# The second token half of a second DFT, done as four extra chunk pairs of a fast block product, with token forms summed in DRAM

## The chip, the core and the metric

The kernel runs on one core of one Trainium2 chip. The metric is the device time of one execution in microseconds, as the median of three runs: 2019.68 us for the kernel before (2019.68 to 2019.91). The engines are named as in the profile: PE multiplies matrices, DVE and ACT do elementwise work, POOL (GpSimd) does elementwise work and issues accumulating transfers, SP issues plain transfers.

## The reference

`x` is 2048 tokens by 512, in fp32. Two branches are mixed per token by a gate:

```
g = sigmoid((x * gate_w).sum(-1))
a = x @ Wd_re.T ; b = x @ Wd_im.T            # DFT along the hidden axis
A = Ws_re @ a - Ws_im @ b                    # DFT along the tokens, real part
logits = x @ w_gate ; gates = softmax(all 8 logits)
B = sum over e of gates[e] * (silu(x @ w1[e]) @ w2[e])     # 8 experts, 512 -> 1376 -> 512
out = g * A + (1 - g) * B
```

All eight experts take every token (top 8 of 8), so the expert branch is two dense products with 8 x 1376 = 11008 inner rows, that is 86 chunks of 128.

## The kernel before

**Precision.** Every fp32 operand is split into a high part (ACT copies it to the reduced type `F32R`) and a low part (DVE or POOL subtracts the high part from the source). `mm` then issues three matmuls for each product, high by high, low by high and high by low, one matmul in each of L349, L352 and L353. A tile of [128 x 512] or [128 x 1024] therefore costs one ACT and one DVE instruction before PE may read it.

**Stages on PE.** One, the token DFT, in eight phases (`phases`, `plan_left_x`, `plan_right`, `dft`); it comes first here, its results `u` (real and imaginary part, four token blocks of 512) go to DRAM as `ud`, and 10 small matmuls (`warm`, `WARM`) run on constant data before the first operands have landed. Two, the hidden DFT (`plan_y`): for each of the four token blocks `gi`, 8 row blocks of `u` (4 real, 4 imaginary) by 4 output blocks by 3 matmuls, 96 matmuls a token block; DVE multiplies the results by `g` and stores them in `yd`. Three, the expert's first product in 29 rounds (`plan_round`) of three chunks each (two in the last): a fast 20-product scheme on blocks; it reads 20 forms of `x` (`XFORM`, blocks of `x` or sums and differences of two blocks), which are made once, during the hidden DFT and the first round, and stay in SBUF. ACT applies silu, DVE multiplies by the gate rows, and four kinds of hidden activations go to DRAM as `hd`. Four, the expert's second product: pairs of chunks (43 of them) in a seven-product scheme (`FORMS`, numbers 1 to 7 in four groups `GROUPS`), each product with two token halves `hf` and two output row blocks `n`, 3 matmuls each. `add_to` adds the seven products into eight accumulators, which start from `yd`; `store` writes them out.

**What sets the order.** The token DFT's events have times written by hand (`ev`). From the hidden DFT on, `Plan` puts every instruction into an order by a list schedule: each has a due time, a duration constant, a release time and buffers from rings (`XF`, `WF`, `RA`, `RW`, `T`, `PS`); tables (`XDUE`, `RAWRING`, `SUMRING`, `NRAW`, `NX`) set due times and rings of the x forms. PE, ACT, DVE and POOL each then run their own instructions strictly in that order; SP issues loads and stores in its order too, and each waits for its buffer.

**Names that the change and the prediction touch.** `xq` is the sum of two x blocks for the token DFT's fifth product, made by DVE in `s1`; `plan_right` sets when the low parts of the DFT matrix are made (`lo`); `raw_block` loads the x blocks for the forms; `add_to` starts an accumulator; `plan_pair_w` and `plan_pair_h` load and split weights and activations for a pair of chunks; `plan_unit` issues a product's matmuls. T1 is the planned start of the rounds, T2 that of the second product.

## Time and profile before

| what | value |
|---|---|
| median of three runs | 2019.68 us |
| the profiled execution, its own time | 2020.08 us |
| its span, first to last instruction | 2018.3 us |
| matmul records on PE | 8836 |
| PE busy | 2006.9 us, 99% |
| DVE / ACT / POOL busy | 1659.0 / 1030.1 / 861.9 us |
| token DFT on PE | to 322.2 us |
| hidden DFT on PE | 322.2 to 409.2 us |
| 29 rounds | 409.2 to 1194.6 us |
| second product | 1194.6 to 2013.5 us |

PE matmuls are pipelined; what counts for the time is the distance of their starts, not the length of a record. The waits are idle time on an engine, put down to the instruction that released it. PEclk in a table of stretches is the share of TensorE's full clock that was granted.

### The profile page before, as it was taken

The numbers are of one execution on the slowest core, as the hardware profiler recorded it, in microseconds if no ns is written. First come the engines' busy times: TensorE is split into PE (matmuls) and PEld (weight loads), VectorE is DVE, ScalarE is ACT, GpSimd is POOL, SyncE is SP. The second block draws the span as 40 slices with busy tenths as digits, with TensorE's granted clock in tenths as the row PEclk, the third lists the DMA queues.
The fourth block names the chain that finished last, engine by engine and source line by source line (L and its number), as shares of the span: only waits on it lengthen the run. The fifth ranks groups of instructions, "written<-read, shape, count | busy, mean of one in ns | idle before, by whom it ended". The sixth has DMA issues, their size and how long they took to land. (4 is left out here: it accounts for less than half of the span.)

```text
span 2018.3 us, 26838 instructions
## 1 busy us (share of the span) xinstructions
PE 2006.9 (99%) x8836; PEld 1655.3 (82%) x8836; DVE 1659.0 (82%) x1929; ACT 1030.1 (51%) x1440; POOL 861.9 (43%) x829
## 2 busy tenths in 40 slices
PE   9999999999999999999999999999999999999999
PEld 7887888888888888888878888888888888888887
DVE  8998996887878887887778786687778888899875
ACT  6544453455555555555555565544445444445442
POOL 0000000188889888889798830000002221235330
PEclk9999999999999999999999999999999999999999
DMA  8676696545565546454645599899889988999991
GB/s 317 214 254 237 221 311 214 190 148 183 175 201 172 185 157 213 166 190 166 221 152 178 178 317 368 298 333 287 268 265 286 293 269 262 279 279 331 303 291 45
DMA packets 205236, 475.20 MB, mean 235 GB/s; under 512 B 22788, under 2 KB 37508, under 8 KB 205096
## 3 DMA queue, kind: packets, MB, share of 16 engines
q1 hardware_dynamic: 192280, 450.15, 64.9%
q0 software_dynamic: 12672, 23.07, 6.9%
q8 instruction: 69, 1.13, 0.2%
q14 instruction: 71, 0.58, 0.1%
q10 hardware_dynamic: 144, 0.26, 0.1%
HBM read 366.36 MB, written 107.03 MB: 235 GB/s over the span
## 5 line engine op out<-in xcount | busy, mean ns | idle before, releaser
L1198 ACT ACTIVATE psp<-psp 128x512 f32<-128x512 f32 x280 | 160.3, 582 | 208.5 <-DVE psp L1182 141.8
L1182 DVE TENSOR_TENSOR psp<-psp,tc 128x512 f32<-128x512 f32 x79 | 55.3, 699 | 33.9 <-PE psp L353 27.9
L1260 ACT ACTIVATE tc<-psp 128x512 f32<-128x512 f32 x88 | 52.4, 597 | 42.7 <-PE psp L353 32.9
L1097 POOL TENSOR_TENSOR tc<-ras 128x256 f32<-128x256 f32 x27 | 20.0, 739 | 121.9 <-DMA ras<-w_dram 120.4
L1427 POOL DMA_DIRECT2D xfx1n<-w_dram x11 | 9.9, 963 | 132.3 <-DVE xf211n L1484 94.8
L1260 ACT ACTIVATE tg<-psp 128x512 f32<-128x512 f32 x67 | 40.0, 598 | 35.4 <-PE psp L353 27.3
L1182 DVE TENSOR_TENSOR psp<-psp,tg 128x512 f32<-128x512 f32 x52 | 36.3, 699 | 21.8 <-PE psp L353 17.8
L340 POOL TENSOR_TENSOR c73011l<-cb,c73011h 128x1024 fp32r<-128x1024 f32 x1 | 2.4, 2412 | 116.8 <-ACT c73011h L346 116.8
L1112 POOL TENSOR_TENSOR wfs1nn<-tc,wfs1nn 128x512 fp32r<-128x512 f32 x32 | 42.0, 1313 | 15.4 <-ACT wfs1nn L1110 8.9
L1208 DVE TENSOR_TENSOR tc<-psp,tc 128x512 f32<-128x512 f32 x62 | 42.5, 685 | 5.2 <-ACT psp L1198 4.2
L1097 POOL TENSOR_TENSOR tc<-tc,ras 128x256 f32<-128x256 f32 x54 | 43.1, 797 | 4.2 <-DVE xfx13n L997 1.8
L1112 POOL TENSOR_TENSOR wfs3n<-tc,wfs3n 128x512 fp32r<-128x512 f32 x29 | 38.4, 1326 | 10.9 <-ACT wfs3n L1110 10.9
L1112 POOL TENSOR_TENSOR wfs2n<-tc,wfs2n 128x512 fp32r<-128x512 f32 x29 | 39.0, 1344 | 8.2 <-ACT wfs2n L1110 8.1
L346 ACT ACTIVATE c<-cd 128x512 fp32r<-128x512 f32 x32 | 20.2, 633 | 38.7 <-DVE cd L343 38.7
L1260 ACT ACTIVATE tw<-psp 128x512 f32<-128x512 f32 x41 | 24.5, 597 | 30.3 <-PE psp L353 23.3
L1182 DVE TENSOR_TENSOR psp<-psp,tw 128x512 f32<-128x512 f32 x37 | 25.9, 699 | 16.4 <-PE psp L353 14.4
L1112 POOL TENSOR_TENSOR wfs0n<-tc,wfs0n 128x512 fp32r<-128x512 f32 x26 | 35.3, 1356 | 7.8 <-ACT wfs0n L1110 7.4
L349 PE MATMUL psp<-xfx,wfs0n 128*128 128x512 f32 x94 | 36.6, 389 | 0.0
L353 PE MATMUL psp<-xfx,wfs0n 128*128 128x512 f32 x94 | 36.6, 389 | 0.0
L340 POOL TENSOR_TENSOR c12111l<-ca,c12111h 128x1024 fp32r<-128x1024 f32 x1 | 2.6, 2602 | 78.4 <-PE u L353 78.4
L1112 POOL TENSOR_TENSOR wfs0n<-tg,wfs0n 128x512 fp32r<-128x512 f32 x24 | 32.1, 1339 | 7.4 <-ACT wfs0n L1110 7.4
L1112 POOL TENSOR_TENSOR wfs3n<-tg,wfs3n 128x512 fp32r<-128x512 f32 x24 | 33.0, 1373 | 3.4 <-ACT wfs3n L1110 3.3
(3474 smaller groups left out, 7980.9 us busy)
## 6 DMA issues: line engine op xcount, KB each, us to landing
hd<-tc SPq DMA_DIRECT2D x161, 256.0 KB, 2.3
ca<-cT_dram SPq DMA_DIRECT2D x63, 512.0 KB, 5.4
hd<-tg SPq DMA_DIRECT2D x108, 256.0 KB, 2.5
hd<-tw SPq DMA_DIRECT2D x75, 256.0 KB, 2.3
...
```

Source lines behind the costliest of these rows:

```text
L340: pin(nc.gpsimd.tensor_tensor(*a))
L346: pin(nc.scalar.activation(dst, src, f, **kw))
L349: ins = nc.tensor.matmul(ps, lh, rh, start=start, stop=False, skip_group_check=True)
L353: nc.tensor.matmul(ps, ll, rh, start=False, stop=stop, skip_group_check=True)
L1097: pin(ins.tensor_tensor(low(b, j), src(x), src(y), o))
L1112: lambda: pin(nc.gpsimd.tensor_tensor(r(w)[:, 1, :], f(b), f(w)[:, 0, :], sub)), [oh] + deps, [b, w],
L1182: q = op("DVE", V, due, lambda: pin(nc.vector.tensor_tensor(f(dst), f(a[0]), f(b_[0]), o)), [a[1], b_[1]] + list(deps), [dst, a[0], b_[0]] ...
L1198: os = op("ACT", A, due, lambda: pin(nc.scalar.activation(f(dst), f(src_), AF.Silu, scale=sign)), [o0], [dst, src_])
L1208: oh = op("DVE", V, due + 1.2, lambda: pin(nc.vector.tensor_tensor(f(hb), f(dst), f(gb), OP.mult)), [os, og], [hb, dst, gb], lock=dst.ring ...
L1260: o = op("ACT", AP_, after(x), lambda: pin(nc.scalar.activation(f(b), f(bank[x[0]]), AF.Copy)), [prod[x]], [b, bank[x[0]]])
L1427: return op("POOL", 0.9, due, lambda: pin(nc.gpsimd.dma_start(f(src_)[:, j, :], block(key), accum_op=add, max_dma_last_dim=4096)), deps, [ ...
```

## The change

The four parts, in the order of the program:

- **Start.** 17 warm-up matmuls instead of 10. In the first phase of the token DFT, the sum `xq` of chunks 4 to 7 is made by a plain load from SP and an accumulating transfer from POOL, instead of a DVE instruction. The low parts of the DFT matrix are given an earlier time in all chunks of this phase, not in one alone.
- **x forms.** Twelve of the twenty forms are sums of two blocks. Each is now written to DRAM once (`xs`): a DRAM-to-DRAM copy from SP, then an accumulating transfer from POOL, spread over the phases from the fourth on. The form is then one load. To have only sums there, signs of forms are moved: into ACT's scale and a DVE scalar_tensor_tensor for the low part, into the weight forms (add becomes sub and the other way round) and into silu's scale.
- **Hidden DFT.** It runs for the first two token blocks only, and ACT copies its results to `yd` without a gate; a DVE multiplication by `g` follows when an accumulator is started. The second token half (blocks 2 and 3) is done in the second expert product: the four row-block pairs of `u`, multiplied by `g`, and the DFT weights are appended as pairs 43 to 46, with `hf` = 1 alone, so 2 units in place of 4 a product (`u_row`, `plan_ht`, `half`). Accumulators of that half start from the first product, by an ACT copy. `TILES` says where the added weight tiles (22, 23, and half of 21) stand in each group.
- **Rounds.** A round of three leftover chunks now holds one mixed chunk and the last chunks of two neighbouring experts.

```diff
-WARM = 10
+WARM = 17
...
-        out += pure[e]
-        if e % 2:
-            out.append(mixed[e // 2])
-    return out + [tuple(rest[-2:])]
+        out += [tuple(e * FULL + 3 * i + j for j in range(3)) for i in range(FULL // 3)]
+        if e % 2 == 0:
+            out.append((E * FULL + e // 2, e * FULL + FULL - 1, (e + 1) * FULL + FULL - 1))
+    return out + [(NCHUNK - 2, NCHUNK - 1)]
...
+
+NPAIR2 = NPAIR + ND
+NB2 = (NPAIR2 + 1) // 2
...
-XFORM = {16: "+21", 6: "+11-21", 7: "+13", 13: "+14", 9: "+22-13", 3: "+22", 0: "-14-21", 10: "+23-22",
-         14: "+21+24", 4: "+13-23", 11: "+14-24", 17: "+13-12", 18: "+13+21", 12: "-11-14",
-         15: "+21+23", 1: "+12-22", 19: "+24-22", 5: "+12-14", 2: "-11-13", 8: "+22-14"}
...
+XFORM = {16: "-21", 6: "+xa", 7: "+13", 13: "+14", 9: "+22-13", 3: "+22", 0: "+21-14", 10: "+xb",
+         14: "+xc", 4: "-xd", 11: "-xe", 17: "+xf", 18: "+13-21", 12: "-xg",
+         15: "+xh", 1: "-xi", 19: "+xj", 5: "-xk", 2: "-xl", 8: "+22-14"}
+
+XSUM = {"xa": ("11", "21"), "xb": ("23", "22"), "xc": ("21", "24"), "xd": ("13", "23"), "xe": ("14", "24"), "xf": ("13", "12"),
...
+NRAW, NX, NRW = 4, 20, 9
...
+TILES = ((*range(9), 22, *range(9, 13), 23, *range(13, 17), 21, *range(17, 21)),
+         (*range(14), 22, *range(14, 17), 23, 17, 18, 21, 19, 20),
+         (*range(9), 22, *range(9, 13), 23, *range(13, 17), 21, *range(17, 21)),
+         (*range(9), 22, *range(9, 13), 23, *range(13, 17), 21, *range(17, 21)))
...
+            if j == 2:
+                v["q"] = xp.tile([P, 256], F32, tag="x", name=f"xq{k}_0")
+                nc.sync.dma_start(v["q"], x[k][:, j, :])
+            else:
+                pin(nc.gpsimd.dma_start(v["q"], x[k][:, j, :], accum_op=add, max_dma_last_dim=4096))
...
+        if k < 4:
+            ev(s5 - 3.3, s1)
+        else:
+            ev(s - 12.5, plus, 2)
+            ev(s - 8.5, plus, 3)
...
+    def x_sum(n, k, blk):
+        d, t = int(blk[0]) - 1, int(blk[1]) - 1
+        src_ = xT[2 * d:2 * d + 2, :, t * GT:(t + 1) * GT]
+        if k == 0:
+            nc.sync.dma_start(xs[n], src_)
+        else:
+            pin(nc.gpsimd.dma_start(xs[n], src_, accum_op=add, max_dma_last_dim=4096))
...
-                plan_right(pr, c, ph, k, s - 14, s - 2.9, r, lo=s - 3.4 if k == 2 else None)
+                plan_right(pr, c, ph, k, s - 14, s - 2.9, r, lo=s - 3.4)
...
+        if (pr, c, ph) == (0, 1, "Y"):
+            for n, blocks in enumerate(XSUM.values()):
+                for k, blk in enumerate(blocks):
+                    ev(T + XSUM_AT[0] * n + XSUM_AT[1] * k, x_sum, n, k, blk)
...
-    T1 = T + NG * TG
+    T1 = T + 2 * TG
...
-            oy = op("DVE", V, end + 1 + 0.8 * q,
-                    lambda q=q, t=t: pin(nc.vector.tensor_tensor(f(t), f(banks[q]), f(gy), OP.mult)),
-                    [o, og], [t, gy, banks[q]])
...
+            oy = op("ACT", AP_, end + 1 + 0.8 * q,
+                    lambda q=q, t=t: pin(nc.scalar.activation(f(t), f(banks[q]), AF.Copy)), [o], [t, banks[q]])
...
-    for gi in range(NG):
+    for gi in range(2):
...
+    def x_block(blk):
+        if blk in XSUM:
+            return xs[list(XSUM).index(blk)]
...
+    def second(dst, src, hi, neg):
+
+        if neg:
+            return nc.vector.scalar_tensor_tensor(dst, src, -1.0, hi, OP.mult, sub)
+        return nc.vector.tensor_tensor(dst, src, hi, sub)
...
-            oh = op("ACT", A2 if k is None else A, xdue[m] - 1.4, lambda h=h, s_=s_, k=k: pin(
-                nc.scalar.activation(r(h) if k is None else r(h)[:, k, :], part(s_, k), AF.Copy)),
+            oh = op("ACT", A2 if k is None else A, xdue[m] - 1.4, lambda h=h, s_=s_, k=k, neg=neg: pin(
+                nc.scalar.activation(r(h) if k is None else r(h)[:, k, :], part(s_, k), AF.Copy, scale=-1.0 if neg else 1.0)),
...
+            sign = -sign if j == 1 else sign
...
+    for gi in (2, 3, 0, 1):
+        g = Buf("T")
+        gates2[gi] = (g, load(T2 + 6, lambda g=g, gi=gi: gate_row(f(g), slice(0, P), E, gi), MB, bufs=[g], rel=T2))
...
+            if hf == 0:
+                oy = load(due - 16, lambda: nc.sync.dma_start(f(b), yd[i, a]), 2 * MB,
+                          deps=[ydone[i, a, n] for n in range(2)], bufs=[b], rel=due - 30)
+                g, og = gates2[a]
+                oy = op("DVE", V2, due - 10, lambda: pin(nc.vector.tensor_tensor(
+                    f(b), f(b), f(g)[:, None, :].to_broadcast([P, 2, GT]), OP.mult)), [oy, og], [b, g], lock=True)
+                acco[hf, i, a] = [[oy], [oy]]
+        if not acco[hf, i, a][n]:
+            q = op("ACT", AP_, due, lambda: pin(nc.scalar.activation(acc(hf, i, a, n), f(src), AF.Copy,
+                                                                     scale=1.0 if o == add else -1.0)),
...
+    order2 = [[p for q in tiles for p in (2 * q, 2 * q + 1) if p < NPAIR2] for tiles in TILES]
...
+    def u_row(n, k, dst, due, rel):
+
+        c, d, (k, a) = n // 2, 2 * (n % 2), k
+        g, og = gates2[2 + a]
+        b, view = dst
+        o = load(due - 6, lambda: nc.sync.dma_start(view(), ud[c, 2 + a, d + k]), MB, bufs=[b], rel=rel)
+
+        def go():
+            if c:
+                pin(nc.vector.scalar_tensor_tensor(view(), view(), -1.0, f(g), OP.mult, OP.mult))
+            else:
+                pin(nc.vector.tensor_tensor(view(), view(), f(g), OP.mult))
+
+        return op("DVE", V, due, go, [o, og], [b, g], lock=True)
+
+    def plan_ht(n, rel, t):
+        bs = [Buf("T") for _ in range(3)]
+        o = [u_row(n, k, (b, lambda b=b: f(b)), t, rel) for b, k in zip(bs, ((0, 1), (0, 0), (1, 1)))]
+        for k in (1, 2):
+            o[0] = op("DVE", V, t + k, lambda k=k: pin(nc.vector.tensor_tensor(f(bs[0]), f(bs[0]), f(bs[k]), sub)),
+                      [o[0], o[k]], [bs[0], bs[k]], lock=True)
+        hdone[3, NPAIR + n] = load(t + 4, lambda: nc.sync.dma_start(ht[n], f(bs[0])), MB, deps=[o[0]], bufs=[bs[0]])
+
+    for n in range(ND):
+        plan_ht(n, T2 + HT_AT[0] + HT_AT[1] * n, T2 + HT_AT[2])
...
+        half = p >= NPAIR
+        v, a = (V, A) if half else (V2, A2)
+
+        def part(x):
+            return x[:, 1, :] if half else x
...
+            if half and k < 3:
+                raw[k] = (b, u_row(p - NPAIR, ((0, 0), (1, 0), (1, 1))[k], (b, lambda b=b: part(f(b))), need - 4, need - 24))
+                continue
+            deps = [hdone[k, p]] if half else [hdone[k, p, hf] for hf in range(2)]
+            raw[k] = (b, load(need - 9, lambda b=b, k=k: nc.sync.dma_start(part(f(b)), ht[p - NPAIR] if half else hd[k, p]),
+                              MB if half else 2 * MB, deps=deps, bufs=[b], rel=need - 24))
...
+        units_ = [(hf, n) for hf in range(p >= NPAIR, 2) for n in range(2)]
```

The tables of rings and due times (`RAWRING`, `SUMRING`, `XDUE`) change too, and with them the order from the hidden DFT on. Three places show it.

ACT in the first phase of the token DFT, at chunk 4 (`c` is the DFT matrix, `xl` the x operand, `h` the high part; in brackets the engine or transfer kind that the instruction waits for). Before:

```order
L346 ACTIVATE xl_12_283<-xr_198 128x512 [waits DMAHW1_49]
L346 ACTIVATE c12004h<-ca_203 128x1024 [waits DMAHW7_49]
L346 ACTIVATE xl_4_298<-xq_0_295 128x256 [waits DVE_49]
L346 ACTIVATE c_301<-cd_205 128x512 [waits DVE_49,PE_49,Activation_49]
L346 ACTIVATE xl_12_323<-xr_246 128x512 [waits DMAHW4_49]
L346 ACTIVATE c12005h<-ca_249 128x1024 [waits DMAHW2_49]
```

and now:

```order
L359 ACTIVATE xl_12_297<-xr_207 128x512 [waits DMAHW1_49]
L359 ACTIVATE c12004h<-ca_212 128x1024 [waits DMAHW7_49]
L359 ACTIVATE xl_4_312<-xq_0_231 128x256 [waits DMASW0_49]
L359 ACTIVATE c_316<-cd_214 128x512 [waits DVE_49,PE_49,Activation_49]
L359 ACTIVATE xl_12_338<-xr_257 128x512 [waits DMAHW5_49]
L359 ACTIVATE c12005h<-ca_260 128x1024 [waits DMAHW2_49]
```

The order is the same; the third row waits for POOL's accumulating transfer where it waited for DVE.

DVE at the end of the hidden DFT and in the first round. `xf` names on lines 997, 1014, 1017 and 1020 (978, 979, 1027 now) are x forms and their sums, L908 is the gate multiplication of the hidden DFT, L1182 and L1208 (1218, 1245) belong to the first round. Before:

```order
L997 TENSOR_TENSOR xfw0n<-wfs_3098,xf14n 128x1024
L908 TENSOR_TENSOR tc_2909<-psp_2979,tc_2930 128x512
L1014 SCALAR_TENSOR_TENSOR tc_2911<-tc_2911,tg_3007 128x512
L908 TENSOR_TENSOR tg_3007<-psp_2991,tc_2930 128x512
L1182 TENSOR_TENSOR tc_2909<-psp_2824,tg_3395 128x512
L997 TENSOR_TENSOR xf12nn<-wfs_3236,xf30n 128x1024
L1020 TENSOR_TENSOR xf15n<-tc_2911,xf13n 128x512
L1017 TENSOR_TENSOR tc_2999<-tc_2999,tg_3418 128x512
```

and now:

```order
L978 SCALAR_TENSOR_TENSOR xf16n<-xfx6n,xf14n 128x1024
L979 TENSOR_TENSOR xf17n<-xf10n,xfx_2986 128x1024
L1218 TENSOR_TENSOR tg_3266<-psp_2861,tg_3255 128x512
L978 SCALAR_TENSOR_TENSOR xfx6nn<-xf11n,xf231nn 128x1024
L1245 TENSOR_TENSOR tc_3059<-psp_3044,tc_3057 128x512
L1218 TENSOR_TENSOR tg_3255<-psp_2869,tc_3237 128x512
L1027 TENSOR_TENSOR wfs_2919<-wfs_2919,xf15n 128x1024
L1218 TENSOR_TENSOR psp_3040<-psp_3040,tg_3314 128x512
```

The gate multiplications are gone from DVE here. Ahead of the first round's own instructions stand 17 of the 20 forms in both; behind its first one follow three forms and one sum now, four instructions of full width, where seven stood, six of them of half width.

DVE in the last group of the second product (L1473 or 1572 sums two kinds of activations, L1484 or 1582 makes a low part, L1449 or 1538 that of a weight tile, L1486 multiplies a row block of `u` by `g`). Before:

```order
L1473 TENSOR_TENSOR xfw4n<-xfx2n,xfw4n 128x1024
L1484 TENSOR_TENSOR xf11n<-xfx2n,xf17n 128x1024
L1484 TENSOR_TENSOR xf12nn<-xfw5n,xf15n 128x1024
L1473 TENSOR_TENSOR xfx12n<-xfx1n,xfx12n 128x1024
L1449 TENSOR_TENSOR xfx13n<-xf31nn,xf211n 128x1024
```

and now, at an added pair:

```order
L1582 TENSOR_TENSOR xf13nn<-xfw3n,xf231nn 128x1024
L1486 SCALAR_TENSOR_TENSOR xfw5n<-xfw5n,tw_3335 128x512
L1572 TENSOR_TENSOR wfs3nnn<-xfw5n,wfs3nnn 128x512
L1572 TENSOR_TENSOR xf201nn<-ras1n,xf201nn 128x1024
L1582 TENSOR_TENSOR xf230n<-wfs3nnn,xf11nn 128x512
L1582 TENSOR_TENSOR xf221n<-xfx0n,xfx7n 128x1024
```

An added pair has instructions of half the width, and one more of them, the multiplication by `g`.

## Rows read from the trace of the kernel before

**Rows 1.** The page's busy times: engine, busy us, share of the span, instructions.

```profile
PE 2006.9 (99%) x8836; PEld 1655.3 (82%) x8836; DVE 1659.0 (82%) x1929; ACT 1030.1 (51%) x1440; POOL 861.9 (43%) x829
```

**Rows 2.** The waits of PE over the whole span: line and output waited with, releaser, us in total, times, longest.

```profile
PE u L619 <- ACT c L346: 2.1, 1, 2.1
...
PE psp L349 <- ACT tc L1260: 1.0, 1, 1.0
PE psp L353 <- POOL wfs2n L1112: 0.7, 1, 0.7
PE psp L349 <- ACT tg L1260: 0.6, 1, 0.6
PE u L349 <- DVE s L343: 0.4, 1, 0.4
PE psp L349 <- ACT tw L1260: 0.4, 1, 0.4
PE u L352 <- DVE c12003l L343: 0.3, 1, 0.3
```

**Rows 3.** The timeline of PE at the end of the program: start, length, line, operands.

```profile
2009.04 0.39 PE L353 MATMUL psp<-xfx10n,xfw 128*128 128x512 f32 x1
...
2013.12 0.39 PE L353 MATMUL psp<-xf10n,xf13n 128*128 128x512 f32 x1
```

**Rows 4.** The timeline of PE in the first 24 us, neighbouring records of one kind merged (x gives their count); idle time before them and its releaser in brackets.

```profile
1.15 3.88 PE L631 MATMUL warm<-one 128*128 128x128 f32 x20 [1.15 <-POOL one L628]
7.16 10.07 PE L619 MATMUL u<-c,xl 128*128 128x512 f32 x36 [2.13 <-ACT c L346]
17.07 0.39 PE L349 MATMUL u<-c12002h,xl 128*128 128x512 f32 x1
...
21.15 0.39 PE L349 MATMUL u<-c12003h,xl 128*128 128x512 f32 x1
21.80 0.50 PE L352 MATMUL u<-c12003l,xl 128*128 128x512 f32 x1 [0.27 <-DVE c12003l L343]
```

**Rows 5.** Stretches of 1 us at the start: stretch, length, busy time of each engine with instructions started (PE, PEld, DVE, ACT, POOL), granted clock, DMA share, GB/s.

```profile
4.00:5.00 1.00, 1.00 (x9) 0.84 (x7) 0.00 (x0) 0.00 (x0) 0.00 (x0) 1.00 0.69 215
7.00:8.00 1.00, 0.84 (x3) 0.70 (x4) 1.00 (x3) 1.00 (x3) 0.00 (x0) 0.74 1.02 404
8.00:9.00 1.00, 1.00 (x4) 0.81 (x3) 1.00 (x2) 0.34 (x2) 0.00 (x0) 0.50 1.06 406
10.00:11.00 1.00, 1.00 (x4) 0.75 (x3) 1.00 (x3) 0.00 (x0) 0.00 (x0) 0.55 1.03 406
11.00:12.00 1.00, 1.00 (x6) 0.83 (x5) 1.00 (x4) 0.67 (x2) 0.00 (x0) 1.00 1.03 416
```

**Rows 6.** The timeline of DVE at the start, the low parts of the DFT matrix for chunks 2, 3 and 4.

```profile
15.12 1.23 DVE L343 TENSOR_TENSOR c12002l<-ca,c12002h 128x1024 fp32r<-128x1024 f32 x1
...
20.53 1.22 DVE L343 TENSOR_TENSOR c12003l<-ca,c12003h 128x1024 fp32r<-128x1024 f32 x1
...
24.14 1.22 DVE L343 TENSOR_TENSOR c12004l<-ca,c12004h 128x1024 fp32r<-128x1024 f32 x1
```

**Rows 7.** The timeline of ACT at chunk 4 of the start: the high part of `xq` and, two instructions on, that of the DFT matrix of chunk 5.

```profile
23.66 0.42 ACT L346 ACTIVATE xl<-xq 128x256 fp32r<-128x256 f32 x1 [0.82 <-DVE xq L343]
...
25.40 1.05 ACT L346 ACTIVATE c12005h<-ca 128x1024 fp32r<-128x1024 f32 x1
```

**Rows 8.** Transfers of the first 45 us by kind, issuing queue, count, size and median us from issue to landing.

```profile
xr<-x_dram SPq DMA_DIRECT2D x4, 256.0 KB, 6.0
```

**Rows 9.** The same from 1200 us on: weight blocks loaded by SP, and blocks added to them by accumulating transfers from POOL.

```profile
xfx1n<-w_dram SPq DMA_DIRECT2D x18, 256.0 KB, 5.2
...
xfx1n<-w_dram POOLq DMA_DIRECT2D x11, 256.0 KB, 7.5
```

**Rows 10.** The timeline of POOL in the second product: the time that an accumulating transfer takes on POOL to be issued.

```profile
1285.45 0.87 POOL L1427 DMA_DIRECT2D xf31nn<-w_dram  x1 [5.41 <-DMA xf31nn<-w_dram]
```

**Rows 11.** Longer stretches, columns as in Rows 5: the first token block of the hidden DFT, the first round, and three parts of the second product.

```profile
324.00:346.00 22.00, 22.00 (x99) 18.22 (x98) 12.39 (x16) 6.01 (x7) 0.00 (x0) 1.00 0.83 291
412.00:440.00 28.00, 26.97 (x119) 22.03 (x118) 23.51 (x32) 18.21 (x33) 22.37 (x22) 1.00 0.44 137
1550.00:1782.00 232.00, 232.00 (x1025) 192.15 (x1025) 196.20 (x158) 109.22 (x111) 58.35 (x48) 1.00 0.89 270
1782.00:1900.00 118.00, 118.00 (x522) 97.74 (x521) 110.25 (x91) 53.90 (x54) 46.10 (x33) 1.00 1.02 321
1900.00:2013.00 113.00, 113.00 (x500) 93.60 (x499) 81.52 (x72) 44.91 (x44) 25.54 (x22) 1.00 0.63 187
```

**Rows 12.** DVE instructions by line: output and inputs, count, least/median/most ns, first and last start; a [128 x 512] gate multiplication, a [128 x 1024] low part, a [128 x 512] low part and a scalar_tensor_tensor.

```profile
L908 DVE TENSOR_TENSOR tc<-psp,tc x10: 676/688/692, 342.1 to 409.0; 128x512 f32<-128x512 f32 x10
...
L1484 DVE TENSOR_TENSOR xf14n<-xfw4n,xf221n x3: 1219/1226/1226, 1230.7 to 1263.9; 128x1024 fp32r<-128x1024 f32 x3
...
L1449 DVE TENSOR_TENSOR xf15n<-xfw5n,xf221n x1: 686/686/686, 1208.4 to 1208.4; 128x512 fp32r<-128x512 f32 x1
...
L1014 DVE SCALAR_TENSOR_TENSOR tc<-tc,tg x2: 685/956/1228, 409.6 to 410.2; 128x512 f32<-128x512 f32 x2
```

**Rows 13.** The timeline at pair 8 of the second product's first group: DVE makes its low part, PE takes it up.

```profile
1212.64 1.22 DVE L1484 TENSOR_TENSOR xfw<-xfx12n,xf13n 128x1024 fp32r<-128x1024 f32 x1
...
1216.39 0.39 PE L349 MATMUL psp<-xf13n,xf211n 128*128 128x512 f32 x1
```

More of the change, by code (lines that the diff above doesn't have):

```diff
@@ L996, in fnet_moe_kernel @@
                 dep, [h, s_], rel=xdue[m] - XDUE[5])
[L997 to L998 removed]
+            last = op("DVE", V2 if k is None else V, xdue[m], lambda l=l, h=h, s_=s_, k=k, neg=neg: pin(second(
+                r(l) if k is None else r(l)[:, k, :], part(s_, k), part(h, k), neg)), [oh, last], [l, h, s_], lock=True)
@@ L1021, in x_half @@
+        neg = terms[0][0] == "-"
+        oh = op("ACT", A, xdue[m] - 1.4, lambda: pin(nc.scalar.activation(
+            r(h)[:, k, :], f(qa), AF.Copy, scale=-1.0 if neg else 1.0)), [os], [h, qa])
+        return op("DVE", V, xdue[m], lambda: pin(second(r(l)[:, k, :], f(qa), f(h)[:, k, :], neg)), [oh],
                   [l, h, qa], lock=True)
@@ L1397, in store @@
              bufs=[accb[hf, i, a]])
-    SKEW, NEARLY = 2, 0
-    units = []
-    for gi, ms in enumerate(GROUPS):
-        for p in range(NPAIR):
-            units.append((gi, 0, p))
-            before = (gi, p - SKEW) if p >= SKEW else (gi - 1, NPAIR + p - SKEW)
-            if before[0] >= 0 and len(GROUPS[before[0]]) == 2:
-                units.append((before[0], 1, before[1]))
-    units += [(len(GROUPS) - 1, 1, p) for p in range(NPAIR - SKEW, NPAIR) if len(GROUPS[-1]) == 2]
-    need_at = {u: T2 + 4 * UNIT * n for n, u in enumerate(units)}
+    SKEW = 2
@@ new lines, in fnet_moe_kernel @@
+    need_at, t = {}, T2
+    for u in units:
+        need_at[u] = t
+        t += UNIT * (4 if u[2] < NPAIR else 2)
+    def u_row(n, k, dst, due, rel):
[9 more added lines that the diff above has]
+        return op("DVE", V, due, go, [o, og], [b, g], lock=True)
```

171 lines of the change are left out of this document (84 added, 87 removed).

## The prediction

> **What bounds the kernel now.** I read the busy times first: PE works for 2006.9 of 2018.3 us, no other engine for more than 83% [rows 1]. The waits of PE then say how little is left to win beside its work: seven waits of 2.1, 1.0, 0.7, 0.6, 0.4, 0.4 and 0.3 us, 5.5 us in all, and none of them in the second product [rows 2]. So the time is the number of matmuls times the distance of their starts, plus these waits, plus a fixed end. The distance is read from the end of the program: from 2009.04 to 2013.12 us there are 18 steps [rows 3], (2013.12 - 2009.04) / 18 = 0.2267 us. Of PE's 8836 records [rows 1] 20 are the warm-up [rows 4] and 16 small ones for the gate; the other 8800 at this distance alone give 1995 us. The start is the one place where the distance is another: 36 matmuls take from 7.16 to 17.07 us, 9.91 us [rows 4], where 36 x 0.2267 = 8.16 us would do. The stretches show why: the granted clock falls to 0.74, 0.50 and 0.55 between 7 and 11 us, its low level of 1.2 GHz, and stands at 1.00 ahead of it and behind it [rows 5]; what came before the fall is PE's 2.13 us of idleness between the warm-up and the first operands [rows 4]. That costs 9.91 - 8.16 = 1.75 us.
>
> The profiled execution took 2020.08 us, its span 2018.3, so 1.8 us lie outside; the median of the runs is 0.4 us below it. The terms below are differences, and I apply them to the median.
>
> **The matmuls, the sure part.** Removed are two token blocks of the hidden DFT, 2 x 96 = 192 matmuls. Added are 7 products x 4 pairs x 2 units x 3 = 168. 24 fewer, x 0.2267 [rows 3] = 5.4 us. PE has no other work under which they could be hidden, so this is on the path as a whole, unless a wait takes their place.
>
> **The start.** Seven more warm-up matmuls leave 14 more records; nine of them start per us at the full clock, between 4 and 5 us [rows 5], so the warm-up ends some 14/9 = 1.6 us later, at 5.03 + 1.6 = 6.6 us [rows 4]. The first operand comes at 7.16 as before, and the idle time is 0.55 us. Idle times of 1.0 us later in the program, such as the one in the first round [rows 2], leave the clock at 1.00 [rows 11]; so I expect the fall to go, and up to 1.75 us with it. But DVE feeds this stretch. At the full clock PE would come to chunk 2 at about 15.5 us, and its low part is ready at 15.12 + 1.23 = 16.35 [rows 6]: a wait of 0.7 us. It reaches chunk 3 at about 20.3 instead of 21.15 [rows 4], where the low part, now made ahead of two other DVE instructions, is ready at about 20.8: another 0.3. At chunk 4 PE is then 24.75 against 25.75 now (21.15 + 0.53 of waiting + 18 x 0.2267): 1.0 us won of the 1.75.
>
> Against that stands the new wait at chunk 4. ACT's high part of `xq` waits for POOL's accumulating transfer, and behind it on ACT, in its order, are the high parts of chunk 4's and chunk 5's DFT matrix. Now that instruction starts at 23.66 and the last of those ends at 25.40 + 1.05 = 26.45 [rows 7]. The load ahead of the accumulation stands eighteenth in SP's order, behind 7.2 MB in a queue that moves about 405 GB/s and is at 215 still in the fifth us [rows 5]: 17.9 us after a start of some 3.5, so it lands near 21.5; POOL needs 0.9 us to issue [rows 10] within the transfer's own time. No row shows an accumulating transfer in this stretch. From below: as fast as PE can use it, 3 us. From above: 7.5 us, as a transfer of twice the size takes in the second product [rows 9]; a plain one of twice the size takes 6.0 here [rows 8]. At 3 us all is in time and the 1.0 us stays won. At 7.5 it lands at 29.0, and ACT's rows behind it put the low part of chunk 5 at 32.7, where PE would want it at 29.0: 3.7 us, which is the 1.0 us and 2.7 more. I take 5 us, between the 6.0 of a plain transfer of twice the size and half of the 7.5: then chunk 5's low part is ready at 30.0 and the 1.0 us is given back. **The start: 0, from -1.0 to +2.7.** On later chunks the same chain has more than 4 us a chunk and DVE one instruction less, so nothing is late there.
>
> A rule speaks to this: after the Trainium skill (DMA: Bandwidth & Descriptors, SWDGE vs HWDGE vs iDMA) each transfer engine takes turns between the software queue, POOL's, and the hardware queue, so POOL's transfer need not stand behind SP's backlog; by it the start would be the -1.0, and the whole 2012.7. The trace bears it out in part only: POOL's 7.5 us against SP's 5.2 in one stretch [rows 9].
>
> **x forms and the hidden DFT.** The hidden DFT lasts two token blocks, 43.5 us, instead of 87. DVE's work there: about 25 instructions of [128 x 1024] ahead of the first round, at 1.22 us [rows 12], a few dearer as scalar_tensor_tensor (0.96 against 0.69 for half the width [rows 12]): some 32 us. Before, sixteen gate multiplications of 0.69 [rows 12] and the sums were among them, in twice the time. The load is 32 of 43.5 us less the 8 that the token DFT's last sums take; it fits, barely, and the last forms are wanted only some 26 us into the first round. Transfers: 17 blocks of 0.5 MB, some 18 MB with all else in about 55 us, 330 GB/s; the first token block now runs at 291 GB/s with a DMA share of 0.83 [rows 11]. Tight too, with 15 us or more between a form's due time and its use. I book 0, at worst the +2.7 of a second set of the rounds' waits (below). The twelve sums in DRAM lie in phases that have room on POOL and queue nothing on PE.
>
> **The rounds.** The same matmuls, the same weights, signs moved at no cost. Four of PE's waits are here, 1.0 + 0.7 + 0.6 + 0.4 = 2.7 us [rows 2], all short collisions of ACT, POOL and PE. A new order moves them; the rows do not say where to. The regrouped rounds load fewer gate rows (76 issues against 87 in SP's order). I take back a fifth: **-0.5, from -2.7 to +2.7.**
>
> **The second product.** DVE for an added pair in the last three groups: a multiplication, a sum and two low parts of 0.69 and half a weight tile's 1.22 [rows 12], 3.4 us, where PE needs 12 x 0.2267 = 2.7. A full pair: three of 1.22 and half a tile, 4.3, against 5.4. So the added pairs run DVE behind by 0.7 us each, and the full ones win 1.1 back each; with 9 or more pairs made up between the added tiles this is hidden by the work made ahead. That there is work ahead shows in the last group: DVE 93% and DMA 1.02 from 1782 to 1900, then 72% and 0.63 [rows 11]. At the front, four gate rows of 0.26 MB are loaded in a stretch full of transfers, 1.05 MB, 3.3 us at 321 GB/s [rows 11]; pair 8 is made at 1213.9 and used at 1216.4 [rows 13], 2.5 us ahead, and the later ones more. **Booked at 0, from 0 to +3.3**; if the cover is gone, see the second rival.
>
> **Sum.** 2019.7 - 5.4 + 0 - 0.5 = 2013.8; I say 2013.7.
>
> **Rivals.** *The start is late:* the accumulation lands after 7.5 us, ACT stands, PE waits at chunk 5. 2019.7 - 5.4 + 2.7 = 2016.9. For it: a full queue, an in-order ACT. Against it: half the bytes. After the Trainium skill (SBUF, the note on the SWDGE trap) POOL cannot write its descriptors while DVE holds the shared port in some modes, and DVE is busy all through this stretch; that would put the case here. The trace speaks against it: POOL issues in 0.87 us while DVE works [rows 10, 11].
>
> *Added pairs are not covered (slower):* in the three two-product groups each added pair waits for DVE, 3 x 4 x 0.7 = 8 us, and for its transfers: in the last group the lone tile brings 1.57 MB for 2.7 us of PE, at 321 GB/s [rows 11] 4.9 us, the double one 2.1 MB, 6.5 for 5.4, together 3.3, and some 1.7 in each of the other two, 6.7. At worst 15 us: 2019.7 - 5.4 + 15 = 2029. It decides from the point at which no form is ready ahead when an added tile comes. Against it: no wait of PE there now, and a mean need that rises by 2% only.
>
> *The rounds lose what PE saves:* their waits double, and the form stage adds as much: -5.4 + 2.7 + 2.7, 2019.7.
>
> **Chances.** Forecast 0.70 (2010.5 to 2015.6: all waits of the rounds and the start's 1.0 gone, to 1.9 us more of them); the start late 0.12; the rounds 0.10; added pairs 0.08. The range, 2010.3 to 2018.8, goes from the first bound to most of the second and some of the third. A difference of 0.2%, 4 us, is about what a measurement of this kernel can tell from none: faster means below 2015.6, which holds nearly all of the forecast and a little of the first rival, 0.72; slower is the second rival, 0.08; the rest is 0.20.
>
> **What would show it.** PE's records would number some 8826, 24 fewer matmuls and 14 more of warm-up; the clock at 1.00 from 7 to 11 us and the 36 matmuls in about 8.5 us; ACT's high part of the first accumulated `xq` before 27 us; PE waits of a little over 2 us in the rounds, none behind 1150 us. It is wrong if PE waits in the second product at the added tiles, if the fall of the clock stays, or if the first round waits for x forms.

## The result, and the profile after

The changed kernel takes 2033.92 us (median of 6 runs, 2033.06 to 2038.19) against 2019.8 for the kernel before: ratio 1.0072, 95% interval 1.0059 to 1.0085. It is slower by 14.1 us, where 6.0 us faster was forecast. The profiled execution took 2033.43 us, its span 2031.6.

Waits of PE over the whole span, columns as in [rows 2]:

```profile
PE u L365 <- DVE c12116l L356: 4.3, 1, 4.3
PE u L362 <- ACT c L359: 2.4, 1, 2.4
PE lt L410 <- ACT xs_2h L359: 2.2, 1, 2.2
PE u L362 <- DVE s L356: 1.9, 1, 1.9
PE psp L362 <- ACT tc L1297: 1.4, 2, 0.8
...
PE lt L412 <- DVE xs_2l L356: 1.1, 1, 1.1
PE u L366 <- DVE xl L356: 0.9, 1, 0.9
PE lt L412 <- DVE xs_0l L356: 0.8, 1, 0.8
```

Everything with `u` or `lt` (the gate's small matmuls) is in the token DFT. That is the stage that the prediction booked at nothing. PE's first matmul of the hidden DFT starts at 342.22 us, before at 322.19, and its last of the program at 2026.74, before at 2013.12 [rows 3]:

```profile
342.22 0.39 PE L362 MATMUL psp<-uh,wd 128*128 128x512 f32 x1
```

So the token DFT is 20.0 us longer, and all that follows takes 1684.5 us where it took 1690.9, 6.4 us less. Behind the token DFT the change did what was forecast; within it three times as much was lost.

The start, with a timeline of PE (as [rows 4]) and two stretches of 1 us (as [rows 5]):

```profile
1.15 6.14 PE L655 MATMUL warm<-one 128*128 128x128 f32 x34 [1.15 <-POOL one L652]
7.04 8.69 PE L643 MATMUL u<-c,xl 128*128 128x512 f32 x36
15.57 0.39 PE L362 MATMUL u<-c12002h,xl 128*128 128x512 f32 x1
16.52 0.50 PE L365 MATMUL u<-c12002l,xl 128*128 128x512 f32 x1 [0.56 <-DVE c12002l L356]
...
30.62 0.50 PE L362 MATMUL u<-c,xl 128*128 128x512 f32 x1 [2.36 <-ACT c L359]
```

```profile
8.00:9.00 1.00, 1.00 (x6) 0.78 (x6) 0.93 (x2) 0.32 (x2) 0.00 (x0) 1.00 1.06 402
10.00:11.00 1.00, 1.00 (x6) 0.83 (x5) 1.00 (x3) 0.00 (x0) 0.00 (x0) 1.00 0.99 383
```

The fall of the clock between 7 and 11 us is gone, and the 36 matmuls take 15.57 - 7.04 = 8.5 us, as expected. PE comes to chunk 4 at 24.98 us, 0.8 us sooner than before (25.79), where 1.0 was forecast. At chunk 5 it then waits 2.4 us. POOL and ACT there:

```profile
23.20 1.01 POOL L512 DMA_DIRECT2D xq<-x_dram  x1 [22.10 <-DMA xq<-x_dram]
```

```profile
23.04 1.05 ACT L359 ACTIVATE c12004h<-ca 128x1024 fp32r<-128x1024 f32 x1
29.63 0.42 ACT L359 ACTIVATE xl<-xq 128x256 fp32r<-128x256 f32 x1 [5.54 <-DMA xq<-x_dram]
29.95 0.61 ACT L359 ACTIVATE c<-cd 128x512 fp32r<-128x512 f32 x1
30.47 0.61 ACT L359 ACTIVATE xl<-xr 128x512 fp32r<-128x512 f32 x1
30.99 1.04 ACT L359 ACTIVATE c12005h<-ca 128x1024 fp32r<-128x1024 f32 x1
```

The plain load lands at 23.2, the accumulation 6.4 us later; ACT stands for 5.5 us and all of chunk 5 stands behind it.

Now the later phases. From 118 to 322 us, before (first row) and after (second), columns as in [rows 5]:

```profile
118.00:322.00 204.00, 203.60 (x898) 165.32 (x898) 189.67 (x236) 99.89 (x116) 14.55 (x10) 1.00 0.72 242
```

```profile
118.00:322.00 204.00, 193.20 (x831) 154.22 (x831) 176.56 (x224) 94.09 (x111) 25.10 (x22) 0.98 0.91 286
```

The first row is the one that the prediction should have read: DVE is busy for 189.67 of 204 us, 93%. From 20 to 125 us it was busy for 98% in the kernel before:

```profile
20.00:125.00 105.00, 104.34 (x459) 85.82 (x458) 103.00 (x157) 58.90 (x79) 4.78 (x2) 1.00 0.68 242
```

From 118 us on the DMA share goes from 0.72 to 0.91. What DVE waits for from 20 to 325 us is now loads, and ACT in the first phases (before, the longest of its waits for a load there was 0.8 us):

```profile
DVE cd L356 <- DMA cd<-cT_dram: 14.1, 4, 11.2
DVE c L356 <- ACT c L359: 7.7, 5, 4.6
DVE cd L356 <- DMA ca<-cT_dram: 5.4, 2, 4.8
```

The longest one, in the timeline of DVE, and the matmul that stands behind it:

```profile
284.16 0.69 DVE L356 TENSOR_TENSOR cd<-cd,ca 128x512 f32<-128x512 f32 x1 [11.24 <-DMA cd<-cT_dram]
...
285.37 1.22 DVE L356 TENSOR_TENSOR c12116l<-ca,c12116h 128x1024 fp32r<-128x1024 f32 x1
```

```profile
286.65 0.80 PE L365 MATMUL u<-c12116l,xl 128*128 128x512 f32 x1 [4.28 <-DVE c12116l L356]
```

During that wait the granted clock falls to its low level, 1.2 GHz, and it stays there until 292 us (0.54 in the mean from 285 to 290 us), which adds to the loss:

```profile
285.00:290.00 5.00, 3.35 (x8) 2.68 (x9) 5.00 (x8) 3.73 (x8) 0.00 (x0) 0.54 0.54 193
```

In the second product nothing waits, at the added pairs or elsewhere. The last two stretches, beside those of [rows 11]:

```profile
1782.00:1900.00 118.00, 118.00 (x522) 97.73 (x521) 107.75 (x93) 57.92 (x60) 43.36 (x38) 1.00 1.01 312
1900.00:2013.00 113.00, 113.00 (x500) 93.55 (x499) 93.98 (x76) 50.46 (x52) 30.02 (x26) 1.00 0.76 235
```

### The profile page after: what moved, and what is told of

Its sections match the earlier page's. It is cut to its first block, busy times and chain, and to the rows that moved or that the text cites. A ratio compares the mean times of both kernels' runs of the same rounds, so it can differ in the third digit from the quotient of the medians.

```text
span 2031.6 us, 27019 instructions
## 1 busy us (share of the span) xinstructions
PE 2008.9 (99%) x8826; PEld 1652.0 (81%) x8826; DVE 1673.7 (82%) x1956; ACT 1052.1 (52%) x1479; POOL 882.2 (43%) x857
## 4 chain that ended last, share of the span: by engine, by line
PE 84%; DMA 1%; DVE 0%; issue 0%; ACT 0%; ACTq 0%; DVEq 0%
PE psp L362 27%; PE psp L366 27%; PE psp L365 27%; PE u L362 1%; PE u L366 1%; PE u L365 1%; DMA hd<-tc 0%; DMA hd<-tg 0%; DVE psp L1218 0%; DVE tc L1218 0%; DVE psp L1268 0%; ACT tc L1297 0%; DVE tc L1245 0%; DVE tg L1245 0%; DVE tw L1245 0%
## 5 line engine op out<-in xcount | busy, mean ns | idle before, releaser
L1148 POOL TENSOR_TENSOR wfs0n<-tc,wfs0n 128x512 fp32r<-128x512 f32 x35 | 47.9, 1369 | 23.5 <-ACT wfs0n L1146 16.2
L770 POOL DMA_DIRECT2D xs<-xT_dram x12 | 10.7, 896 | 102.0 <-DMA xs<-xT_dram 56.0
L1148 POOL TENSOR_TENSOR wfs3nn<-tc,wfs3nn 128x512 fp32r<-128x512 f32 x32 | 42.8, 1336 | 15.0 <-ACT wfs3nn L1146 14.7
L1297 ACT ACTIVATE tw<-psp 128x512 f32<-128x512 f32 x52 | 31.0, 598 | 29.1 <-PE psp L366 21.4
L1148 POOL TENSOR_TENSOR wfs1n<-tc,wfs1n 128x512 fp32r<-128x512 f32 x29 | 39.4, 1360 | 9.8 <-ACT wfs1n L1146 9.8
L1148 POOL TENSOR_TENSOR wfs2nn<-tc,wfs2nn 128x512 fp32r<-128x512 f32 x29 | 38.2, 1317 | 7.3 <-ACT wfs2nn L1146 7.3
L356 DVE TENSOR_TENSOR cd<-cd,ca 128x512 f32<-128x512 f32 x32 | 24.1, 755 | 19.4 <-DMA cd<-cT_dram 14.1
L1133 POOL TENSOR_TENSOR tc<-ras,tc 128x256 f32<-128x256 f32 x40 | 35.8, 903 | 2.0 <-DVE tc L1271 1.4
L365 PE MATMUL psp<-xfx,wfs1n 128*128 128x512 f32 x88 | 34.3, 389 | 0.0
L365 PE MATMUL psp<-xfx,wfs0n 128*128 128x512 f32 x88 | 34.2, 389 | 0.0
```

What stands on the lines that cost most here:

```text
L356: pin(nc.vector.tensor_tensor(*a))
L365: nc.tensor.matmul(ps, lh, rl, start=False, stop=False, skip_group_check=True)
L770: pin(nc.gpsimd.dma_start(xs[n], src_, accum_op=add, max_dma_last_dim=4096))
L1133: pin(ins.tensor_tensor(low(b, j), src(x), src(y), o))
L1148: lambda: pin(nc.gpsimd.tensor_tensor(r(w)[:, 1, :], f(b), f(w)[:, 0, :], sub)), [oh] + deps, [b, w],
L1297: o = op("ACT", AP_, after(x), lambda: pin(nc.scalar.activation(f(b), f(bank[x[0]]), AF.Copy)), [prod[x]], [b, bank[x[0]]])
```

## The experiments

All are edits of the changed kernel. Times are medians; the kernel before ran at 2019.6 to 2020.3 us beside them. "Hidden DFT" is the start of its first matmul in the profiled execution, "rest" the time from there to the start of PE's last matmul: before 322.2 and 1690.9 us. The runs without sums, and e3, e10 and e11, leave out one of the two blocks of each of the twelve forms: they tell what a part costs and are no versions of the kernel. Whole computations are the change, e1, e6 and e14.

| run | low parts | xq of chunks 4 to 7 | x sums | us | hidden DFT | rest |
|---|---|---|---|---|---|---|
| the change | early | POOL | in DRAM | 2033.9 | 342.2 | 1684.5 |
| e1 | early | DVE | in DRAM | 2038.1 | 349.5 | 1683.5 |
| e2 | early | POOL | none | 2019.8 | 329.2 | 1682.8 |
| e3 | early | POOL | copies alone | 2022.0 | 330.8 | 1683.5 |
| e4 | early | DVE | none | 2018.0 | 328.2 | 1684.6 |
| e5 | as before | DVE | none | 2012.4 | 322.2 | 1683.7 |
| e6 | as before | DVE | in DRAM, spread | 2025.4 | 334.5 | 1683.1 |
| e7 (10 warm-ups) | as before | DVE | none | 2012.0 | 322.2 | 1683.8 |
| e10 | early | POOL | POOL, plain | 2031.4 | 342.1 | 1683.2 |
| e11 | early | POOL | 24 copies on SP | 2031.5 | 342.2 | 1682.9 |
| e12 | as before | POOL | none | 2017.2 | 326.9 | 1682.9 |
| e13 (10 warm-ups) | as before | DVE | on the chip (see below) | 2029.4 | 322.1 | 1700.8 |
| e14 (10 warm-ups) | as before | DVE | on the chip | 2027.5 | 322.1 | 1699.8 |

**One cause at a time.** e1 undoes the accumulating `xq`, e2 leaves the sums out, e3 keeps the copies alone, e4 is e1 and e2 together.

```
-        if k < 4:
+        if k < 8:                                  # e1, e4
             ev(s5 - 3.3, s1)
...
-                for k, blk in enumerate(blocks):
+                for k, blk in enumerate(blocks[:0]):   # e2, e4; blocks[:1] in e3
...
-            return xs[list(XSUM).index(blk)]
+            blk = XSUM[blk][0]                     # e2, e4
```

> The changed kernel with one edit undone: the sums xq of chunks 4 to 7 are made by DVE again; 17 warm-up matmuls, the earlier low parts and everything else stay. Theory: in the changed kernel PE waits 2.5 us for chunk 5 and 1.1 us in the five-products of chunks 5 and 7 because ACT stands behind the accumulating transfer; without it the 5.0 us by which the first phase ends later than before go, and the 0.6 to 0.8 us won up to chunk 4 stay: 2033.9 - 5.5 = 2028.4. Rival: the loss comes from DVE's new order (the low parts earlier, the sums later), which stays: 2033 or so, with PE still waiting at chunk 5.

> The changed kernel without the twelve sums of x in DRAM: neither the copies nor the accumulating transfers are issued, and each of the twelve forms loads the first of its two blocks instead (left out: the second block of these forms). Theory: the transfers of the sums fill the transfer engines in the last five phases of the token DFT (DMA share 0.92 to 1.05 where it was 0.52 to 0.85), loads of the DFT matrix land late, and PE's waits there, some 15 us with the fall of the clock at 286 us, go: 2033.9 - 15 = 2019. Rival: the waits come from something else that moved (the order of SP's issues, DVE's order), and the time stays above 2030.

> The changed kernel with the twelve copies from DRAM to DRAM on SP, but without POOL's twelve accumulating transfers (left out: the second block of twelve forms). Theory, room in the transfer engines: the accumulating transfers take 17.6 of the engines' time in a hundred from 100 to 322 us, the copies less; so most of the 15 us goes, 2033.9 - 10 = 2024, with 2 to 5 us left at places where the load was above 0.9 anyway. Rival one, POOL's queue or its writing of descriptors is what harms: the same time as without the sums at all, about 2019. Rival two, the copies in SP's order hold up the loads behind them: 2030 or more.

> The changed kernel without the sums in DRAM (each of the twelve forms loads one block alone: left out) and with xq made by DVE. If the two causes add up and there is no third: 2033.9 - 15 - 5.5 = 2013.4, which is what the rest of the change is worth, 2019.8 less 24 matmuls at 0.2267 us and about a us of waits in the rounds and at the start. If the rest of the change has a cost of its own that these waits hid, 2016 or more.

e2 gives 2019.8: the sums cost 14.1 us. Matmul by matmul, the change falls behind e2 in two places: 3.7 us from 169 to 193 us (the gate's small matmuls) and 8.5 us from 278 to 304 us (at and behind `c12116l`). e3 gives 2022.0: the copies alone 2.3. e1 missed: 2038.1, slower by 4. Its second phase starts 2.3 us sooner than the change's, at 44.6 against 46.9, but at 131 us the two are level: behind the wait at 123 us the clock falls in e1 (0.70 from 125 to 130 us), in the change it stays at 1.00. It falls again in e1 at 190 us, and PE waits more in the later phases (5.5 us at `c12116l`); which collision of transfers does that was not tried. e4 missed by 4.6: 2018.0, so a third cause was left. PE waits for DVE, 1.6 us at 44 and 1.9 at 123 us, although DVE waits for no load up to there. The third place, which the expectation of e5 puts at 140 us, is no wait but the clock: it stands at its low level from 124 to 127 us, which costs 1.6 us:

```profile
124.00:127.00 3.00, 3.00 (x9) 2.38 (x8) 3.00 (x6) 0.00 (x0) 3.00 (x2) 0.54 0.01 5
```

**The third cause, the warm-up, the place and the queue.** e5 is e4 with the low parts put back, e7 takes the warm-up back as well; e6 has the whole computation with the sums spread; e10 makes POOL's transfers plain.

```
-                plan_right(pr, c, ph, k, s - 14, s - 2.9, r, lo=s - 3.4)
+                plan_right(pr, c, ph, k, s - 14, s - 2.9, r, lo=s - 3.4 if k == 2 else None)   # e5, e6, e7
...
-WARM = 17
+WARM = 10                                          # e7
...
-                    ev(T + XSUM_AT[0] * n + XSUM_AT[1] * k, x_sum, n, k, blk)
+                    ev(XSUM_AT[n] - (0 if k else 12), x_sum, n, k, blk)     # e6, from the first phase
+XSUM_AT = (66, 76, 86, 98, 112, 128, 146, 162, 180, 240, 252, 302)
...
-            pin(nc.gpsimd.dma_start(xs[n], src_, accum_op=add, max_dma_last_dim=4096))
+            pin(nc.gpsimd.dma_start(xs[n], src_, max_dma_last_dim=4096))    # e10
```

> The run without the sums in DRAM and with xq made by DVE (e4; of twelve forms one block is left out), and now the low parts of the DFT matrix at their times of before as well (early at chunk 2 alone); 17 warm-up matmuls stay. In e4 6.0 us are still lost by the second phase of four: PE waits at 42, 119 and 140 us for DVE, which has no idle time of its own from 20 to 125 us except 5.6 us in which it waits for ACT's high part of the differences c, seven times up to 1.4 us. Before, the low part stood between the difference and that wait and covered it. Theory: the order of the low parts is this third cause; DVE's 5.6 us go to 1 and PE's 6.0 us go: 2018.0 - 6 = 2012, the first phase ends where it did before or up to a us sooner. Rival: the loss comes from the earlier start of PE (17 warm-ups) into a stretch where the transfers are full; then PE still waits there, and the time is 2016 or more.

> As the run with the low parts as before (e5; no sums in DRAM, of twelve forms one block left out), with 10 warm-up matmuls instead of 17. It tells what the warm-up alone is worth. By the prediction's working the clock falls again between 7 and 11 us, which costs 1.75 us at the 36th matmul, of which DVE's feed gives back 0.7: 1.0 us slower than e5 at the end. Rival: DVE, which has no idle time until 125 us, sets when the second and the fourth phase can go on, so that what PE wins in the first 17 us is waited away by 120 us: the same time as e5.

> The whole computation: the changed kernel with xq made by DVE and the low parts as before, and the twelve sums in DRAM spread from the second phase to the end of the token DFT, instead of from the fourth to the seventh phase. Between 40 and 320 us the transfer engines of the kernel before were idle for some 82 us of 280 (mean share 0.71), the twelve accumulating transfers took 39 and the copies less than 20. Theory, it is the room in the engines at each place: spread, most of the 15 us of the sums go, 4 to 6 remain where the share was above 0.8 anyway: 2012 + 5 = 2017. Rival: each accumulating transfer costs about a us wherever it is, by the time it takes from the loads in a stretch where DVE has no slack: 2012 + 12 = 2024 or more.

> The changed kernel with POOL's twelve transfers issued at the same places, of the same size, but plain, without adding to what stands in DRAM (left out: the sums; of twelve forms the second block alone is kept). Theory: an accumulating transfer takes the engines longer than a plain one of its bytes (3.3 us of all sixteen for 0.5 MB, against some 1.5), so plain ones cost little more than the copies alone: 2022 + 2 = 2024. Rival: it is POOL's queue itself, beside SP's loads, or the number of transfers, that delays the loads: 2030 or more, near the changed kernel's 2033.9.

e5 came out as expected, 2012.4 (ratio 0.9962, 0.9947 to 0.9977); that is faster than the kernel before, but it loads one block where twelve forms need two. Why the order of the low parts counts is seen at chunk 3 in DVE's timeline, first after, then e5:

```profile
19.71 1.22 DVE L356 TENSOR_TENSOR c12003l<-ca,c12003h 128x1024 fp32r<-128x1024 f32 x1
20.85 0.42 DVE L356 TENSOR_TENSOR xq<-xr 128x256 f32<-128x256 f32 x1
21.18 0.69 DVE L356 TENSOR_TENSOR cd<-cd,ca 128x512 f32<-128x512 f32 x1
22.65 0.69 DVE L356 TENSOR_TENSOR c<-cd,c 128x512 fp32r<-128x512 f32 x1 [0.78 <-ACT c L359]
```

```profile
19.97 0.68 DVE L356 TENSOR_TENSOR cd<-cd,ca 128x512 f32<-128x512 f32 x1
20.57 1.21 DVE L356 TENSOR_TENSOR c12003l<-ca,c12003h 128x1024 fp32r<-128x1024 f32 x1
21.70 0.68 DVE L356 TENSOR_TENSOR c<-cd,c 128x512 fp32r<-128x512 f32 x1
```

DVE makes the difference `cd`, ACT its high part, DVE the low part `c`. The long instruction used to lie between the two and covered ACT's time; moved ahead, it leaves DVE idle for 0.8 us at each of chunks 3 to 6 and for 1.4 at chunk 7 (e4; before, at chunk 2 alone). DVE has no slack until 125 us: of the 105 us from 20 us on it is busy for 103.00 in e5 as before, and for 99.01 in e4. So PE pays later.

e7 is as fast as e5: the seven warm-ups are worth nothing. In e7's profiled execution, with ten warm-ups and 1.3 us of idle time ahead of the 36 matmuls, the clock did not fall in this stretch, so e7 does not tell what the fall costs; e5 against the kernel before does. PE in e5 at chunk 3:

```profile
20.44 0.39 PE L362 MATMUL u<-c12003h,xl 128*128 128x512 f32 x1
21.84 0.50 PE L365 MATMUL u<-c12003l,xl 128*128 128x512 f32 x1 [1.01 <-DVE c12003l L356]
```

Before, the two stood at 21.15 and 21.80, with a wait of 0.27 [rows 4]; DVE made `c12003l` at 20.53 [rows 6], in e5 at 20.57. PE comes 0.7 us sooner and waits 0.7 us longer.

e6 missed: 2025.4 (ratio 1.0028, 1.0019 to 1.0037), 13 us above e5; its rival was right, about a us for each sum at these places too. e10 missed too: plain transfers cost 2031.4, not 2024, though they hold the engines for half as long; its rival (2030 or more) was right. After and e10, POOL's queue from 100 to 322 us (packets, MB, share of 16 engines):

```profile
q0 software_dynamic: 3264, 6.29, 17.6%
```

```profile
q0 software_dynamic: 1728, 6.29, 9.2%
```

**Bytes or the queue, and the fourth of four.** e11 has SP make both copies, into two tensors (`nc.sync.dma_start((xs, xs2)[k][n], src_)`, in place of POOL's); e12 is e2 with the edit of e5.

> The changed kernel with the second blocks of the twelve sums copied by SP too, plainly and into a DRAM tensor of their own that nobody reads, instead of POOL's accumulating transfers (left out: the second block of twelve forms). It moves as many bytes as the run with plain transfers from POOL (e10, 2031.4), in one queue. Theory, the bytes: DVE is 95% busy in the token DFT, the transfers share the engines with its loads, and 12.6 MB more cost what they cost in e10, whoever issues them: 2029 or more. Rival, the second queue: a transfer of POOL's queue takes turns with SP's loads and holds them up, while the same transfer in SP's own order only stands behind them: twice the 2.3 us that the twelve copies alone cost (2022.0 against 2019.8 without them), 2024 to 2025.

> Without the sums in DRAM (of twelve forms one block is left out), the low parts of the DFT matrix at their times of before, 17 warm-ups, and xq of chunks 4 to 7 by POOL's accumulating transfer, as in the change. It is the fourth of four: low parts early and xq by POOL 2019.8, low parts early and xq by DVE 2018.0, low parts as before and xq by DVE 2012.4. If the two edits of the start add up, 2012.4 + 1.8 = 2014.2. If the accumulating transfer is late by itself (issued at 23.2 us, landed at 29.6, with ACT's rows for chunk 5 behind it), the 2.5 us of PE's wait at chunk 5 and what follows in DVE's order stay: 2015 to 2017.

e11 decides between the queues: 2031.5, as e10, without POOL. It is the copies on the transfer engines, in either queue; whether their bytes or their number counts was not told apart. They do not add up evenly: the first twelve copies cost 2.3 us, twelve more 9.5. The stretch from 118 to 322 us, e3 and then e11:

```profile
118.00:322.00 204.00, 201.80 (x885) 162.58 (x885) 190.29 (x236) 100.13 (x116) 14.59 (x10) 1.00 0.79 270
```

```profile
118.00:322.00 204.00, 195.65 (x834) 156.42 (x834) 179.99 (x225) 95.07 (x111) 14.57 (x10) 0.97 0.82 286
```

In e3 DVE is as busy as before; in e11 it loses 10 us, and PE 6. DVE's waits for the loads of `cd` from 20 to 325 us, e3 and then e11:

```profile
DVE cd L356 <- DMA cd<-cT_dram: 2.8, 3, 1.9
```

```profile
DVE cd L357 <- DMA cd<-cT_dram: 10.5, 5, 3.9
```

e12 gives 2017.2: the accumulating `xq` alone costs 4.8 us, at the upper end of what was expected of the late landing by itself (2015 to 2017). PE waits 2.4 us at chunk 5, and then the clock stands at its low level until 35 us:

```profile
32.00:35.00 3.00, 3.00 (x8) 2.15 (x8) 3.00 (x5) 2.40 (x5) 0.89 (x1) 0.50 1.09 366
```

At chunk 6 PE is 4.6 us behind e5 (38.63 against 33.98) and stays so. The early low parts alone cost 5.6 (e4 against e5), both 7.4 (e2 against e5). They do not add up to 10.4. In part that is the clock: its fall at 124 us costs e4 1.6 us, and in e2 it does not fall. For the rest, DVE waits for ACT at chunk 5 for 6.0 us in e12 and for 5.2 in e2, so the one late landing seems to take in the idle time that the early low part leaves at that chunk; this was not tried by itself.

**The sums on the chip.** e13 and e14 load both blocks of a form in the hidden DFT and add them there, in halves, with a new order, new rings and new due times of the forms. e13 makes form 0 in a buffer that form 13 still has to read; in e14 form 0 waits for it.

```
+            for k in range(2):
+                q = Buf("T")
+                o = load(due - XDUE[6] - ONCHIP[2], lambda q=q, k=k: nc.sync.dma_start(f(q), more[k]), MB, bufs=[q],
...
+                out.append(op("POOL" if on else "DVE", G if on else V, due - ONCHIP[1],
+                              lambda q=q, k=k, eng=eng: pin(eng.tensor_tensor(half(k), half(k), f(q), add)),
...
```

> The whole computation: the changed kernel with the start as before (10 warm-ups, low parts and xq as before) and without the sums in DRAM; instead the two blocks of each of the twelve forms are loaded in the hidden DFT and the first round and added on the chip, 22 half additions by DVE, 2 by POOL, with new due times and rings for the forms. Without any sums (e7) it is 2012.0. From 288 to 388 us DVE is busy for 76.6 of 100 us there, so 23 us are free, and the additions take 22 x 0.69 = 15; twelve more loads of 0.5 MB at 321 GB/s take 20 us, where the share of 0.71 leaves 29. Theory, there is room: the time is 2012 plus a few us of collisions, 2017, ahead of both kernels. Rival, the room lies at the wrong places: the first round wants one form after the other from 43 us after the token DFT on, and what is late there PE waits for: 15 us or more, 2027, so that the sums cost the same 14 us wherever they are made.

> The same with one dependence more, so that a form is not made in the buffer of a block before the last other form of that block has been read (in e13 form 0 is made in block 14's buffer ahead of form 13's low part, which changes form 13; the work is the same). In e13 PE waited 3.7, 3.5, 2.4 and 1.4 us for forms and for u at 358 to 398 us, and the clock fell to 0.79 there. If those waits are the price of the room at the wrong places, they stay: 2027 to 2031. If they came from the wrong order, 2020 or less.

e13 took 2029.4, e14 2027.5 (ratio 1.0037, 1.0022 to 1.0051), 15.5 us above e7, so the rival was right. The token DFT is as short as before, and the rest 16 us longer than without sums. PE's waits in e14, and the two stretches in which they lie, at the end of the hidden DFT and in the first round:

```profile
PE psp L366 <- DVE xf32nnn L1002: 3.7, 1, 3.7
PE psp L366 <- DVE xfw2n L917: 3.5, 1, 3.5
PE psp L363 <- ACT xf230n L915: 2.3, 1, 2.3
PE psp L366 <- DVE xf13nn L1003: 1.2, 1, 1.2
```

```profile
358.00:368.00 10.00, 4.24 (x15) 2.95 (x14) 8.71 (x7) 5.57 (x7) 7.89 (x5) 0.88 1.03 361
398.00:410.00 12.00, 7.29 (x21) 5.47 (x22) 10.11 (x10) 3.82 (x6) 10.77 (x9) 0.72 0.29 107
```

In the first DVE is at 8.7 of 10 and the transfers at 1.03, in the second DVE is at 10.1 and POOL at 10.8 of 12: room in the mean of 100 us was no room in the stretches that count. None of the versions with the sums in it (the change, e1, e6, e14) beats the kernel before.

## Why the prediction was wrong

- **"The twelve sums in DRAM lie in phases that have room on POOL and queue nothing on PE"**: this step failed, by 14.1 us of the 20 that the forecast is off (e2 against the change). POOL had room, but the transfer engines and DVE hadn't. 12.6 MB share the engines with the loads of the DFT matrix; DVE, 93% busy, waits for the loads, cannot catch up, and PE waits for DVE. The prediction looked for what is queued on PE and POOL alone. The row of DVE and DMA for the token DFT was never read.
- **"The start: 0, from -1.0 to +2.7"** failed by 7.4 us (e2 against e5). Of its parts: the clock's fall went, as forecast, and of the 1.0 us to be won at chunk 4 the change had 0.8. But that gain hung on the early order (a low part ready at "about 20.8"; it was 20.9), and in e5, with the order of before, it is gone by chunk 3, into the wait for `c12003l`. The accumulation was to land 5 us after its issue: it took 6.4, and its load came 1.7 us later than the 21.5 forecast, so ACT's high part came at 29.63, not before 27 and later than the 29.0 of the upper bound. This is the first rival's mechanism; alone it costs 4.8 (e12), where 2.7 was its bound. PE's wait at chunk 5, 2.4 us, was about what the bound allowed; the bound ended there, and behind it came the clock's fall in e12 and further waits for DVE in the change (0.9 us at 46 us, 1.9 at 125). The early low parts were booked as help; alone they cost 5.6, by uncovering ACT's time.
- **"On later chunks ... DVE one instruction less, so nothing is late there"**: wrong for the same reason. DVE's idle time is what counts up to 125 us, and it rose.
- **The matmuls, -5.4, and the rounds, -0.5**: right. The rest of the program takes 6.4 us less in the change and 6.3 to 8.1 less in the runs without the sums on the chip. PE's waits in the rounds fell from 2.7 [rows 2] to 1.8 us, in e5 to 1.2. The 0.5 was a guess (the rows did not say where the waits would go), so that it came near is luck; the 24 matmuls are not.
- **The second product, 0, and the x-form stage, 0**: right while the sums come from elsewhere; the one wait up to the end of the first round is 0.6 us in the change. The second rival (added pairs not covered) didn't come. The sums made in that stage (e14) break the second booking.
- **POOL's queue.** The Trainium skill (DMA: Bandwidth & Descriptors, SWDGE vs HWDGE vs iDMA) has each transfer engine take turns between the software and the hardware queue; the prediction gave it as a rule by which the 1.0 us at the start would stay won. No such gain shows: 128 KB took 6.4 us in POOL's queue, and the same bytes cost the same in either queue (e10 2031.4, e11 2031.5); whether the engines took turns no run shows. The rule of the Trainium skill (SBUF — State Buffer, SBUF: two separate sides) that POOL cannot write its descriptors while DVE holds the shared port in some modes was rightly left aside: POOL issued in 0.9 to 1.0 us, the first time with DVE at work (23.26 us).

What stays open: which transfers collide in e1 and not in the change, what makes the clock fall behind a wait in one run and not in another, and why the second twelve copies cost four times the first. The clock is a part of the last: in e11's profiled execution it falls at 30, 125, 195 and 295 us, in e3's at 30 us alone.
